# Gate and up half passes of three units in one run, in shared pairs of PSUM banks

## The chip, the core and the metric

The kernel runs on one core of a Trainium2 chip. The metric is device time in microseconds (us) of one execution. The granted TensorE clock was 1.000 in the profiled execution.

## What is computed

`x` is 2048 x 448. Its layer norm `xn` goes through two branches that are added to `x`: a GFNet filter (a two-dimensional FFT, a product with a complex weight, the inverse FFT) and a gated ReLU feed-forward layer with 1792 hidden columns.

```python
xn = _layernorm(x)
X = rfft2(xn) * (w_r + 1j * w_i)
y = irfft2(X, s=(S, D))                     # S = 2048, D = 448
gate = einsum("bsd,df->bsf", xn, W_gate)    # F = 1792
up = einsum("bsd,df->bsf", xn, W_up)
h = gate * (gate > 0) * up
return x + y + einsum("bsf,fd->bsd", h, W_down)
```

## The kernel before

Every product runs in fp16 with each operand split into a high and a low part, so that one product of fp32 operands costs three matmuls (high by high, high by low, low by high).

**Units.** The hidden columns are cut into 14 slabs `f` of 128, the 2048 rows into 4 chunks `q` of 512 (order `CHUNKS`). A gate and up unit is one (`f`, `q`): two accumulations of 128 x 512, gate in one PSUM bank and up in the next, in one tile named `gu` of shape 128 x 2 x 512 (one bank holds 512 fp32). The slabs stand in three groups of 5, 5 and 4. That makes 56 units, listed in `gseq` by group, chunk and slab. When all slabs of a group are done for a chunk, four down blocks follow (`dn_mm`), each 128 rows by 448 columns in a PSUM tile `dn`, with 15 matmuls in groups of five slabs and 12 in the group of four.

**Full and half passes.** The contraction over 448 takes, with the splits, ten full passes of 128 rows and one of 64 rows for gate, and the same for up (`gu_full`, L729, 20 matmuls for a unit; `gu_half`, L736, two). A half pass uses half of TensorE's rows. The gate half pass stands in rows 0 to 63, the up half pass in rows 64 to 127 (`TOP`), so the two run side by side.

**Runs.** Half passes of two units stand together. Units are taken in pairs (lead, mate): after the 20 full passes of the lead, `gu_halves` opens the mate's PSUM tile, issues the mate's two half passes with `start`, so they open its accumulation, and then the lead's two with `stop`, so they close it. The mate's 20 full passes follow later. That is a run of four half passes, and 28 such runs in the program.

**PSUM.** There are eight banks: two tiles `gu` of two banks, two tiles `dn` of one bank, two tiles `fx` of one bank for all FFT products.

**Who reads the tiles.** `gu_relu` (ScalarE, L766) reads the gate bank, `gu_times` (VectorE, L770) the up bank; `dn_post` (VectorE, L803) reads a down block and adds it to the result tile `xy`. Only after that can a tile's banks be written again by their next tenant. `gu_hi` (L774) and `gu_lo` (L778) make the fp16 parts `h` for the down blocks.

**What sets the order.** The first 44 us or so follow a list written by hand (`OPENING`); its entries `hp0`, `hp2`, `hp4` are the runs of half passes of the first units. After that a scheduler orders each engine's queue when the program is built: among instructions that its model of the chip finds ready it takes the one of highest priority. Half passes have a raised priority (an offset of 2000) except the first of a run, and each is tied to the one before it in order (`tc.add_manual_dep`, a tie of order, not a wait). FFT work (forward L358 and L399, inverse L619 and L647, and much of VectorE's work) is spread between the units as background. TensorE works its queue off in that order, so once built, nothing moves ahead of a wait.

Of the kernel before, what the change touches and what calls it, by code (L numbers as in the profile page):

```python
# [10 lines left out]
F32 = mybir.dt.float32  # L11
# [11 lines left out]
VT = XW + 14  # L23
GROUPS = [5, 5, 4]
LAG, AHEAD, RAMP = 1, 3, 6
NWARM = 19
N2ORD = [0, 8, 4, 12, 2, 10, 6, 14, 1, 9, 5, 13, 3, 11, 7, 15]
CHUNKS = [0, 2, 1, 3]
# [128 lines left out]
def tile_gfnet_reglu(ctx: ExitStack, tc: tile.TileContext, x, xr, wgu, wd, wf, ident, c_fd, c_fm, c_im, c_row, c_id,  # L157
# [5 lines left out]
    psum = ctx.enter_context(tc.tile_pool(name="psum", bufs=1, space=bass.MemoryType.PSUM))  # L163

    def mt(shape, dt, name, bufs=1):
        return main.tile(shape, dt, name=name, bufs=bufs)
# [44 lines left out]
    state = {}  # L211
# [506 lines left out]
    hps, ht = {}, {}  # L718

    SEQ = [(r + 4 * k, r) for r in range(3) for k in (0, 1)] + [(t, 4 + t) for t in range(3)] + [(3, 3)]  # L720
    TOP = ((slice(0, 64), 3), (slice(64, 128), 7))

    def gu_open(f, q):
        hps[f, q] = psum.tile([128, 2, 512], F32, name="gu", bufs=2)

    def gu_full(f, q, gs, cs, start, stop, seq=SEQ):
        for g in gs:
            for i, (a, b) in enumerate(seq):
                last["P"] = P.matmul(hps[f, q][:, g, cs], wt[f, g][:, a, :], Tq[q][:, b, cs],  # L729
                                     start=(start and i == 0), stop=(stop and i == len(seq) - 1)).ins  # L730

    def gu_half(f, q, g, start, prev):


        rows, b = TOP[g]
        m = P.matmul(hps[f, q][:, g, 0:512], wt[f, g][rows, 7, :], Tq[q][rows, b, :], start=start, stop=not start).ins  # L736
        if "opened" in state:
            tc.add_manual_dep(m, prev.name, NOSYNC, reason="half passes stand together")
        return m

    NOSYNC = mybir.DependencyInfo(mybir.DependencyClass.NoSync, mybir.DependencyReason.DATA)
    opened = set()

    def gu_unit(f, q, mate):

        gs, cs = (0, 1), slice(0, 512)
        if (f, q) in opened:
            gu_full(f, q, gs, cs, False, True)
            return
        gu_open(f, q)  # L750
        gu_full(f, q, gs, cs, True, False)
        gu_halves(f, q, mate)

    def gu_halves(f, q, mate):
        gu_open(*mate)
        m = last["P"]
        for i in range(4):
            with tc.high_priority(offset=2000 if i else 0):
                m = gu_half(*((f, q) if i > 1 else mate), 1 - i % 2, i < 2, m)
        opened.add(mate)  # L760

    g1s = {}

# [16 lines left out]
    def gu_post(f, q):  # L780
        gu_relu(f, q)
        gu_times(f, q)
        gu_hi(f, q)
        gu_lo(f, q)
# [4 lines left out]
    def dn_mm(fs, n2):  # L789
        q, j = n2 % 4, n2 // 4  # L790
        js = slice(128 * j, 128 * (j + 1))
        ps = psum.tile([128, 512], F32, name="dn", bufs=2)
        n = 3 * len(fs)
        i = 0
        for f in fs:
            for a, b in ((0, 0), (0, 1), (1, 0)):
                last["P"] = P.matmul(ps[:, 0:D], ht[f, q][:, a, js], wdt[f][:, b, :], start=(i == 0),  # L797
                                     stop=(i == n - 1)).ins
                i += 1
        dps[n2] = ps  # L800

    def dn_post(g, n2):
        last["V"] = V.scalar_tensor_tensor(xy[:, n2, :], dps[n2][:, 0:D], dsc[:, g:g + 1], xy[:, n2, :],  # L803
                                           op0=OP.mult, op1=OP.add).ins

    def store(n2):

        if n2 in stored:
            nc.sync.dma_start(ov[:, n2, :], xy[:, n2, :])
        stored.add(n2)  # L810
# [111 lines left out]
    for t in range(16 + len(il) - 1):  # L922
# [4 lines left out]
        for st in reversed(range(len(il))):  # L927
            i = t - st
# [14 lines left out]
    def run_bg(until=None, amount=0.0):  # L943
        credit[0] += amount
        while pos[0] < len(bg) and (credit[0] > 0 if until is None else pos[0] < until):
            c, p, fn, a = bg[pos[0]]
            bg_item(fn, a)
            pos[0] += 1
            credit[0] -= c - load[0] * p
# [3 lines left out]
    for n in GROUPS:  # L953
        groups.append(list(range(f0, f0 + n)))
        f0 += n
    gseq = [("gu", g, f, q) for g, fs in enumerate(groups) for q in CHUNKS for f in fs]
    units, pend = [], []
    for k, u in enumerate(gseq):
        units.append(u)
        if k % 2 and pend:  # L960
            units += pend
            pend = []
        if u[2] == groups[u[1]][-1]:
            pend = [("dn", u[1], u[3] + 4 * j, None) for j in range(4)]
    units += pend
    mates = {u: v for u, v in zip(gseq[::2], gseq[1::2])}
    first = {}
    for i, u in enumerate(units):
        if u[0] == "gu" and u[2] not in first:
# [49 lines left out]
    def keep_warm(n):  # L1019
        for _ in range(n):  # L1020
            P.matmul(wps, warm[:, 0:128], warm, start=True, stop=True)

    pieces = {"lid": lambda: nc.sync.dma_start(id_t, ident), "lfd": lambda: nc.sync.dma_start(fd_t, c_fd),
              "lw": load_wn, "warm": lambda: keep_warm(NWARM),
              **{f"kw{n}": (lambda n=n: keep_warm(n)) for n in (1, 3, 6)},
# [3 lines left out]
    def piece(name, fn, *a):  # L1029
        pieces[name] = lambda: fn(*a)  # L1030
# [14 lines left out]
    q = CHUNKS[0]  # L1045

    def gu_slab(f, g):
        if f % 2 == 0 and g == 0:
            gu_open(f, q)
        gu_full(f, q, (g,), slice(0, 512), f % 2 == 0, f % 2 == 1)  # L1050

    for f in groups[0]:
        piece(f"lwd{f}", load_wd, f)
        piece(f"wdq{f}", wd_sq, f, f)
        piece(f"wdh{f}", wd_hi, f, f)
        piece(f"wdl{f}", wd_lo, f, f)
        piece(f"parW{f}", w_sum, f)
        piece(f"wscW{f}", w_scale, f)
        for tag, fn in (("re", gu_relu), ("tm", gu_times), ("gh", gu_hi), ("gl", gu_lo)):
            piece(f"{tag}{f}", fn, f, q)  # L1060
        if f % 2 == 0:
            piece(f"hp{f}", gu_halves, f, q, mates["gu", 0, f, q][2:])
        for g in range(2):
            piece(f"wsqW{f}g{g}", w_sq, f, g)
            piece(f"whiW{f}g{g}", w_hi, f, g)
            piece(f"wloW{f}g{g}", w_lo, f, g)
            piece(f"gu{f}g{g}", gu_slab, f, g)
            if f == 0:
                piece(f"parW{f}g{g}", w_sum, f, (g,))
                piece(f"wscW{f}g{g}", w_scale, f, (g,))  # L1070
                for h in range(2):
                    for tag, sq in (("hh", seq1[0:3]), ("lh", seq1[3:6]), ("hl", seq2)):
                        piece(f"{tag}{g}{h}", gu_full, f, q, (g,), half[h], tag == "hh" and h == 0, False, sq)

    with tc.manual_schedule(engines={mybir.EngineType.PE, mybir.EngineType.DVE, mybir.EngineType.Activation,
                                     mybir.EngineType.SP, mybir.EngineType.Pool}):
        A.activation(mt([128, 1], F32, "root"), eps, AF.Sqrt)
        G.memset(warm, 0.0)
        wps = psum.tile([128, 512], F32, name="dn", bufs=2)
        gu_open(0, q)  # L1080
        for name in OPENING.split():
            pieces[name]()
# [12 lines left out]
    def room(i, share):  # L1095
        return max(0.0, share * took(units[i]) - fixed(i))
# [4 lines left out]
    for _ in range(40):  # L1101
        m = (lo + hi) / 2
# [5 lines left out]
    @contextmanager  # L1108
    def after(i):
        k = max(0, len(anchors) - 1 - i)  # L1110
        with tc.issue_after(anchors[k]), tc.issue_after(act_anchors[k]):
            yield

    for i, u in list(enumerate(units))[len(groups[0]):]:
        is_gu = u[0] == "gu"
        if is_gu:
            _, g, f, q = u
            run_bg(until=marks["T", q])
            gu_unit(f, q, (mates.get(u) or (0, 0, None, None))[2:])
        else:  # L1120
            _, g, n2, _ = u
            dn_mm(groups[g], n2)
        with after(LAG):
            for fn, a in at.get(i, []):
                with tc.high_priority(offset=200):
                    fn(*a)
            for v in units[i + 1:i + 1 + AHEAD]:
                if v[0] == "gu":
                    run_bg(until=marks["T", v[3]])
            run_bg(amount=room(i, load[0]) if i >= RAMP else 0.0)  # L1130
        if is_gu:
            with tc.high_priority(offset=400):
                gu_post(f, q)
        else:
            with tc.high_priority(offset=400):
                dn_post(g, n2)
            if g == len(groups) - 1:
                store(n2)
        anchors.append(last["V"])
        act_anchors.append(last["A"])  # L1140
# [46 lines left out]
```

## Time and profile before

| what | value |
|---|---|
| time, median of 3 runs | 455.11 us (454.88 to 455.12) |
| the profiled execution | span 453.5 us from the first to the last instruction; its own time is not listed, and the runs' median is 1.6 us above its span |
| TensorE (PE) busy | 445.2 us, 98% of the span, 2613 matmuls |
| VectorE (DVE) busy | 383.6 us, 85% |
| ScalarE (ACT) busy | 188.0 us, 41% |
| GpSimd (POOL) busy | 22.5 us, 5% |
| granted TensorE clock | 1.000 |

In the profile's rows PE is TensorE's matmuls and PEld its weight loads, DVE is VectorE, ACT ScalarE. Rows of the timeline give the start, the length from the first start to the last end, engine, line, operation, tile written and tiles read, shapes and the count of matmuls merged into the row. Matmuls are pipelined: a row's length includes the drain of its last matmul, so the pace is read from one row's start to the next row's start. Rows of the groups give the count, the busy time, the mean ns of one, and after the bar the engine's idle time before them with what ended it.

### The profile page before, as it was taken

Reading aid. Unit: us, or ns where it says so; the run is one execution under the profiler, and the core shown is the slowest. Engines: PE = TensorE matmul, PEld = TensorE weight load, DVE = VectorE, ACT = ScalarE, POOL = GpSimd, SP = SyncE. Lnnn points to the kernel's source line nnn. Section 1 sums busy time; section 2 is a strip of 40 time slices with the busy share of each in tenths; the row PEclk is TensorE's granted clock in tenths of the full one; section 3 lists DMA queues with packets and bytes.
Section 4 is the critical chain, followed back from the end, with each engine's and each line's share of the span. In section 5 each row is a group of like instructions: output and inputs, shape, how many; then the busy total and the mean of one; then the engine's idle time right before and its main releaser. Section 6 shows DMA issues by size and latency. Waiting matters only on the chain.

```text
span 453.5 us, 7307 instructions
## 1 busy us (share of the span) xinstructions
PE 445.2 (98%) x2613; PEld 224.9 (50%) x2613; DVE 383.6 (85%) x931; ACT 188.0 (41%) x406; POOL 22.5 (5%) x73
## 2 busy tenths in 40 slices
PE   7999999999999999999999999999999999999996
PEld 2544645555555444444444444444555656655642
DVE  5999798979769799999999999996996989875522
ACT  4896233542544575143124345433263344243020
POOL 2220020100000040000000000000000000000000
PEclk9999999999999999999999999999999999999999
DMA  7939983130001462341320200002210211110202
GB/s 255 324 71 283 382 252 65 25 70 2 1 1 48 138 195 71 92 144 41 88 58 21 82 21 2 0 1 81 68 59 24 93 52 63 58 35 1 103 20 81
DMA packets 36908, 39.39 MB, mean 87 GB/s; under 512 B 16278, under 2 KB 32534, under 8 KB 36872
## 3 DMA queue, kind: packets, MB, share of 16 engines
q1 hardware_dynamic: 36872, 38.93, 27.8%
q8 instruction: 20, 0.33, 0.3%
q14 instruction: 16, 0.13, 0.1%
HBM read 24.69 MB, written 3.67 MB: 63 GB/s over the span
## 4 chain that ended last, share of the span: by engine, by line
PE 95%; DVE 2%; DMA 1%; ACT 1%; SPq 0%; issue 0%
PE gu L729 53%; PE dn L797 28%; PE gu L736 3%; PE fx L647 3%; PE fx L358 3%; PE fx L619 2%; PE fx L399 2%; DMA y<-in_xr 1%; ACT wt L679 0%; ACT T L344 0%; DVE xy L803 0%; DVE bst L261 0%; DVE tt L323 0%; SPq L237 0%; SPq L231 0%
## 5 line engine op out<-in xcount | busy, mean ns | idle before, releaser
L729 PE MATMUL gu<-T,wt 128*128 128x512 f16 (+1 forms) x1140 | 255.3, 375 | 0.0
L729 PEld LDWEIGHTS <-wt 128*128 128x128 f16 x1140 | 109.2, 98 | 128.5 <-issue 8.1
L797 PE MATMUL dn<-wdt,h 128*128 128x448 f16 x672 | 136.4, 352 | 0.6 <-DVE xy L803 0.6
L797 PEld LDWEIGHTS <-h 128*128 128x128 f16 x672 | 65.3, 98 | 61.1 <-issue 1.3
L766 ACT ACTIVATE g<-gu 128x512 f32<-128x512 f32 x56 | 33.3, 595 | 119.2 <-PE gu L736 87.5
L770 DVE SCALAR_TENSOR_TENSOR g<-gu,g 128x512 f32<-128x512 f32 x56 | 38.4, 686 | 23.7 <-ACT g L766 23.4
L774 ACT ACTIVATE h<-g 128x512 f16<-128x512 f32 x56 | 34.9, 626 | 51.3 <-DVE g L770 51.3
L778 DVE TENSOR_TENSOR h<-g,h 128x512 f16<-128x512 f32 x56 | 38.3, 685 | 7.9 <-ACT h L774 7.5
L803 DVE SCALAR_TENSOR_TENSOR xy<-dn,dsc,xy 128x448 f32<-128x448 f32 x48 | 32.4, 678 | 10.8 <-PE dn L797 10.8
L679 ACT ACTIVATE wt<-wst,wsc 128x512 f16<-128x512 f32 x28 | 19.0, 714 | 5.0 <-DVE wsc L207 5.0
L635 ACT ACTIVATE pgh<-pg 114x512 f16<-114x512 f32 x16 | 10.1, 630 | 25.3 <-PE fx L647 20.5
L683 DVE SCALAR_TENSOR_TENSOR wt<-wst,wsc,wt 128x512 f16<-128x512 f32 x28 | 20.3, 745 | 0.1
L197 ACT ACTIVATE junk<-wst 128x512 bf16<-128x512 f32 x28 | 17.5, 623 | 1.9 <-DMA wst<-in_wgu 1.6
L736 PE MATMUL gu<-T,wt 64*128 64x512 f16 x112 | 17.0, 381 | 0.2 <-DVE wt L683 0.2
L647 PE MATMUL fx<-idc_t,pgh 114*128 114x112 f16 (+1 forms) x192 | 16.6, 236 | 0.0
L647 PEld LDWEIGHTS <-pgh 114*128 114x128 f16 x192 | 13.9, 98 | 3.8 <-issue 0.8
L406 DVE TENSOR_TENSOR y<-y,y 128x456 f32<-128x456 f32 x22 | 13.9, 630 | 2.3 <-DMA row<-y 1.8
L652 DVE SCALAR_TENSOR_TENSOR xy<-fx,fsc,xy 128x448 f32<-128x448 f32 x16 | 10.8, 678 | 5.4 <-PE fx L647 5.4
L200 POOL PARTITION_ALL_REDUCE wm<-wm x15 | 6.2, 416 | 176.9 <-ACT junk L197 161.0
L603 ACT ACTIVATE vt<-y,fsc 128x456 f16<-128x456 f32 x16 | 10.8, 672 | 9.2 <-DMA y<-row 5.4
L405 DVE TENSOR_TENSOR y<-y,y 128x456 f32<-128x456 f32 x22 | 13.8, 628 | 0.2
L390 ACT ACTIVATE Xh<-X 128x456 f16<-128x456 f32 x16 | 9.2, 577 | 11.2 <-DVE X L388 6.8
(118 smaller groups left out, 453.7 us busy)
## 6 DMA issues: line engine op xcount, KB each, us to landing
sw<-y SPq DMA_DIRECT2D x64, 112.2 KB
wst<-in_wgu SPq DMA_DIRECT2D x28, 256.0 KB
wf<-in_wf SPq DMA_DIRECT2D x16, 228.0 KB
y<-in_xr SPq DMA_DIRECT2D x16, 224.0 KB
xy<-in_x SPq DMA_DIRECT2D x16, 224.0 KB
out<-xy SPq DMA_DIRECT2D x16, 224.0 KB
wdst<-in_wd SPq DMA_DIRECT2D x14, 224.0 KB
fm<-in_c_fm SPq DMA_DIRECT2D x4, 256.0 KB
```

What stands on the lines that cost most here:

```text
L197: A.activation(mt([128, 512], BF16, "junk")[:, 0:src.shape[-1]], src, AF.Square, scale=SQ, accum_out=acc)
L647: P.matmul(ps[:, o0:o1], h[:, a, i, :], idc_t[:, b, c0:c0 + o1 - o0], start=(j == 0 and i < 3), stop=True, skip_group_check=True)
L679: A.activation(w[:, 0:4, :], wst[f, g], AF.Copy, scale=wsc[f, g])
L683: V.scalar_tensor_tensor(w[:, 4:8, :], st, sc, w[:, 0:4, :], op0=OP.mult, op1=OP.subtract)
L729: last["P"] = P.matmul(hps[f, q][:, g, cs], wt[f, g][:, a, :], Tq[q][:, b, cs], start=(start and i == 0), stop=(stop and i == len(seq) - 1 ...
L736: m = P.matmul(hps[f, q][:, g, 0:512], wt[f, g][rows, 7, :], Tq[q][rows, b, :], start=start, stop=not start).ins
L766: last["A"] = A.activation(g1s[f, q], hps[f, q][:, 0, :], AF.Relu, scale=2.0 ** -22).ins
L770: last["V"] = V.scalar_tensor_tensor(g1, hps[f, q][:, 1, :], 2.0 ** -22, g1, op0=OP.mult, op1=OP.mult).ins
L774: A.activation(ht[f, q][:, 0, :], g1s[f, q], AF.Copy)
L778: V.tensor_tensor(h[:, 1, :], g1s.pop((f, q)), h[:, 0, :], op=OP.subtract)
L797: last["P"] = P.matmul(ps[:, 0:D], ht[f, q][:, a, js], wdt[f][:, b, :], start=(i == 0), stop=(i == n - 1)).ins
L803: last["V"] = V.scalar_tensor_tensor(xy[:, n2, :], dps[n2][:, 0:D], dsc[:, g:g + 1], xy[:, n2, :], op0=OP.mult, op1=OP.add).ins
```

## The change

Units are now taken in batches: 2, 2, then sixteen of 3, then 2, 2 (56 units, 20 batches). The first unit of a batch is the lead, the others are its mates. `gu_halves` opens each mate's tile and issues its two half passes, mate by mate, and the lead's two at the end; all but the very first have the raised priority. The pool `gu` has three tiles of two banks; the pool `dn` is gone, and two down blocks share one `gu` tile, one bank each (`pair_of_banks`). The warm-up matmuls at the start use one such tile as well. Down blocks that are due are put after the end of a batch. Nothing is added or left out: each engine has the same number of instructions as before.

```diff
+BATCHES = [2, 2]
...
+    def pair_of_banks():
+        return psum.tile([128, 2, 512], F32, name="gu", bufs=3)
+
     def gu_open(f, q):
-        hps[f, q] = psum.tile([128, 2, 512], F32, name="gu", bufs=2)
+        hps[f, q] = pair_of_banks()
...
-    def gu_halves(f, q, mate):
-        gu_open(*mate)
+    def gu_halves(f, q, mates):
         m = last["P"]
-        for i in range(4):
-            with tc.high_priority(offset=2000 if i else 0):
-                m = gu_half(*((f, q) if i > 1 else mate), 1 - i % 2, i < 2, m)
-        opened.add(mate)
+        for i, v in enumerate([*mates, (f, q)]):
+            mate = i < len(mates)
+            if mate:
+                gu_open(*v)
+                opened.add(v)
+            for g in (1, 0):
+                with tc.high_priority(offset=0 if not i and g else 2000):
+                    m = gu_half(*v, g, mate, m)
...
     def dn_mm(fs, n2):
...
-        ps = psum.tile([128, 512], F32, name="dn", bufs=2)
+        if j % 2 == 0:
+            state["dn"] = pair_of_banks()
+        ps = state["dn"][:, j % 2, :]
...
+    batches = BATCHES + [3] * ((len(gseq) - sum(BATCHES) - 4) // 3) + [2, 2]
+    assert sum(batches) == len(gseq)
+    lead, ends = {}, set()
+    for n in batches:
+        k = len(ends) and max(ends) + 1
+        lead[gseq[k]] = [v[2:] for v in gseq[k + 1:k + n]]
+        ends.add(k + n - 1)
     units, pend = [], []
     for k, u in enumerate(gseq):
         units.append(u)
-        if k % 2 and pend:
+        if k in ends and pend:
...
-        wps = psum.tile([128, 512], F32, name="dn", bufs=2)
+        wps = pair_of_banks()[:, 0, :]
```

How the built order moves is shown at one place, the third chunk of the second group of slabs (row tile `T1`), on TensorE's queue. Ahead of the change, the unit `gu_2935` is the lead and `gu_2956` its mate (`wt` are weights, `T1` the rows; the number in a name tells tiles apart):

```order
L729 LDWEIGHTS wt_2042
L729 MATMUL gu_2935<-T1_64,wt_2042 128x512
L736 LDWEIGHTS wt_2095
L736 MATMUL gu_2956<-T1_64,wt_2095 128x512
L736 LDWEIGHTS wt_2090
L736 MATMUL gu_2956<-T1_64,wt_2090 128x512
L736 LDWEIGHTS wt_2042
L736 MATMUL gu_2935<-T1_64,wt_2042 128x512
L736 LDWEIGHTS wt_2037
L736 MATMUL gu_2935<-T1_64,wt_2037 128x512
L729 LDWEIGHTS wt_2090
L729 MATMUL gu_2956<-T1_64,wt_2090 128x512
```

The four half passes stand in one run, the lead's full passes ahead of it, the mate's behind it.

With the change, at the same place the batch has the lead `gu_2878` and the mates `gu_2899` and `gu_2902`; `gu_2827` ahead of them is a tile of two down blocks. After the lead's 20 full passes come 30 matmuls of down blocks, and then:

```order
L806 LDWEIGHTS h_2738
L806 MATMUL gu_2827<-wdt_2550,h_2738 128x448
L740 LDWEIGHTS wt_2033
L740 MATMUL gu_2899<-T1_64,wt_2033 128x512
L740 LDWEIGHTS wt_2028
L740 MATMUL gu_2899<-T1_64,wt_2028 128x512
L733 LDWEIGHTS wt_2028
L733 MATMUL gu_2899<-T1_64,wt_2028 128x512
```

and 20 full passes of `gu_2899` later:

```order
L733 MATMUL gu_2899<-T1_64,wt_2033 128x512
L740 LDWEIGHTS wt_2095
L740 MATMUL gu_2902<-T1_64,wt_2095 128x512
L740 LDWEIGHTS wt_2090
L740 MATMUL gu_2902<-T1_64,wt_2090 128x512
L740 LDWEIGHTS wt_1970
L740 MATMUL gu_2878<-T1_64,wt_1970 128x512
L740 LDWEIGHTS wt_1965
L740 MATMUL gu_2878<-T1_64,wt_1965 128x512
L733 LDWEIGHTS wt_2090
L733 MATMUL gu_2902<-T1_64,wt_2090 128x512
```

The six half passes of the batch stand in two runs here, one of two and one of four, with the first mate's full passes between them. So it is in 15 of the 16 batches of three, with 2 to 20 full passes or other work between; in the sixteenth, the one that `OPENING` places, the six stand in one run. The four batches of two have runs of four. That makes 35 runs in the built order, 20 of four or six half passes and 15 of two.

On VectorE's queue at the same place the read of the down block that frees the tile of `gu_2899` stands as follows (`xy` is the result, the lines ahead of it are background FFT work; the first row reads the other tile's first block):

```order
L812 SCALAR_TENSOR_TENSOR xy_61<-gu_2827,dsc_90,xy_61 128x448
L537 TENSOR_TENSOR y2_68<-y2_68,sw2_1921 128x4x57
L538 TENSOR_TENSOR y2_68<-y2_68,sw2_1921 128x4x57
...
L429 SCALAR_TENSOR_TENSOR y16_82<-y4_70,y5_71 128x456
L430 SCALAR_TENSOR_TENSOR y5_71<-y4_70,y5_71 128x456
L504 TENSOR_TENSOR y4_70<-y1_67,wf_2382 128x456
L505 TENSOR_TENSOR y1_67<-y1_67,wf_2382 128x456
L506 TENSOR_TENSOR y4_70<-y4_70,y1_67 128x4x57
L507 TENSOR_TENSOR y4_70<-y4_70,y1_67 128x4x57
L504 TENSOR_TENSOR y1_67<-y11_77,wf_2384 128x456
L505 TENSOR_TENSOR y11_77<-y11_77,wf_2384 128x456
L812 SCALAR_TENSOR_TENSOR xy_61<-gu_2780,dsc_90,xy_61 128x448
```

Left out in it are two more rows like the second and third. Before, a mate's tile was never freed by a down block, since down blocks had banks of their own; now the half passes of a mate wait for this read, the tile `gu_2780` being the former tenant of `gu_2899`'s banks.

More of the change, by code (lines that the diff above doesn't have):

```diff
@@ L742, in tile_gfnet_reglu, with gu_unit @@
     opened = set()
-    def gu_unit(f, q, mate):
+    def gu_unit(f, q, mates):
         gs, cs = (0, 1), slice(0, 512)
@@ L751, in gu_unit @@
         gu_full(f, q, gs, cs, True, False)
-        gu_halves(f, q, mate)
-    def gu_halves(f, q, mate):
-        gu_open(*mate)
+        gu_halves(f, q, mates)
+    def gu_halves(f, q, mates):
         m = last["P"]
-        for i in range(4):
-            with tc.high_priority(offset=2000 if i else 0):
-                m = gu_half(*((f, q) if i > 1 else mate), 1 - i % 2, i < 2, m)
-        opened.add(mate)
+        for i, v in enumerate([*mates, (f, q)]):
[6 more added lines that the diff above has]
+                    m = gu_half(*v, g, mate, m)
     g1s = {}
@@ L965, in tile_gfnet_reglu @@
     units += pend
-    mates = {u: v for u, v in zip(gseq[::2], gseq[1::2])}
     first = {}
@@ L1061, in tile_gfnet_reglu @@
         if f % 2 == 0:
-            piece(f"hp{f}", gu_halves, f, q, mates["gu", 0, f, q][2:])
+            piece(f"hp{f}", gu_halves, f, q, lead["gu", 0, f, q])
         for g in range(2):
@@ L1118, in tile_gfnet_reglu @@
             run_bg(until=marks["T", q])
-            gu_unit(f, q, (mates.get(u) or (0, 0, None, None))[2:])
+            gu_unit(f, q, lead.get(u))
         else:
```

## Prediction

> **What bounds the kernel now.** I read the page's busy times first, then the chain that ended last, then who TensorE waits for, then its timeline around the half passes.
>
> ```profile
> PE 445.2 (98%) x2613; PEld 224.9 (50%) x2613; DVE 383.6 (85%) x931; ACT 188.0 (41%) x406; POOL 22.5 (5%) x73
> core 0: 453.5 us, clock 1.000
> PE 95%; DVE 2%; DMA 1%; ACT 1%; SPq 0%; issue 0%
> PE fx L338 <- DVE tt L323: 1.8, 2, 1.5
> PE dn L1021 <- POOL warm L1078: 1.5, 1, 1.5
> PE dn L797 <- DVE xy L803: 0.6, 1, 0.6
> PE fx L338 <- ACT wt L679: 0.5, 1, 0.5
> PE gu L736 <- DVE wt L683: 0.2, 1, 0.2
> ```
>
> TensorE makes up 95% of the chain. The last five rows are all its waits: 4.6 us, of which all but the 0.6 at L803 belong to the transposes, the warm-up and the first weights at the start. From there to the last chunk it never stands still for another engine. So the time is TensorE's instruction stream plus what is lost between two instructions of that stream, and the change leaves the stream's matmuls as they are in kind and number. What remains is what a run of half passes costs beyond its own passes. The timeline of TensorE shows it:
>
> ```profile
> 29.92 8.81 PE L729 MATMUL gu<-T,wt 128*128 128x512 f16 x40
> 38.66 0.60 PE L736 MATMUL gu<-T,wt 64*128 64x512 f16 x4
> 38.88 0.38 PE L736 MATMUL gu<-T,wt 64*128 64x512 f16 x2
> 39.20 4.49 PE L729 MATMUL gu<-T,wt 128*128 128x512 f16 x20
> 43.52 0.54 PE L797 MATMUL dn<-wdt,h 128*128 128x448 f16 x2
> ...
> 251.88 5.84 PE L797 MATMUL dn<-wdt,h 128*128 128x448 f16 x30
> 257.56 0.59 PE L729 MATMUL gu<-T,wt 128*128 128x512 f16 x2
> 258.08 0.61 PE L736 MATMUL gu<-T,wt 64*128 64x512 f16 x4
> 258.62 4.49 PE L729 MATMUL gu<-T,wt 128*128 128x512 f16 x20
> 262.95 1.68 PE L797 MATMUL dn<-wdt,h 128*128 128x448 f16 x8
> ```
>
> (The third row is a narrow window on the second half of the run in the second.) A full pass has a pace of 0.216 us: 20 of them from 39.20 to 43.52 and again from 258.62 to 262.95. Forty take 8.64, but from 29.92 to the run at 38.66 it is 8.74: **0.10 is lost going in**. At 257.56 two take 0.43, but the run starts 0.52 later: 0.09. The run's first pair starts at 38.66, its second at 38.88: 0.22, the pace of one full pass, so the two half passes of a pair run side by side, and nothing to speak of is lost between pairs. From the second pair at 38.88 to the next full pass at 39.20 is 0.32, which is **0.10 lost going out**. A run of four so takes 0.54 (258.08 to 258.62 as well) where its two passes are worth 0.43, and with the way in it loses 0.21. That holds with a down block ahead or behind:
>
> ```profile
> 277.90 4.48 PE L729 MATMUL gu<-T,wt 128*128 128x512 f16 x20
> 282.31 0.61 PE L736 MATMUL gu<-T,wt 64*128 64x512 f16 x4
> 282.85 5.85 PE L797 MATMUL dn<-wdt,h 128*128 128x448 f16 x30
> 288.54 8.80 PE L729 MATMUL gu<-T,wt 128*128 128x512 f16 x40
> ```
>
> In: 4.41 less 4.32 is 0.09; the run 0.54. Going in and out is paid once a run, however many pairs stand in it. The 28 runs lose 28 x 0.21 = 5.9 us, the largest loss in TensorE's stream.
>
> **The change, part by part.**
>
> *Runs of half passes.* Read from the code, 28 runs become 20 batches, worth 8 x 0.21 = 1.7 us. The built order says otherwise. In 15 of the 16 batches of three, the first mate's pair stands alone, other work follows, and the second mate's pair comes later with the lead's: two runs in place of one. So there are 20 runs of two or three pairs and 15 of a single pair, 35 in all, seven more than before. A run of three pairs costs what one of two does, by the 0.22 between pairs. A run of one pair is not in the trace. Bounds: nothing, if a lone pair could be slipped in free, and 0.21, as for a run of two. I take 0.20, 0.10 in and 0.10 out, since both losses stand at the borders of a run and the borders are the same. Sum: 20 x 0.21 + 15 x 0.20 = 7.2 against 5.9, so **+1.3 us**; with 0.21 for all, 7 x 0.21 = +1.5. I take **+1.4**.
>
> [...]
>
> *PSUM: three pairs that down blocks share.* `gu_times` and `dn_post` cost the same; what changes is who waits for them. A mate's pair now waits for the down block that last held its banks. VectorE works a long queue, and reads late:
>
> ```profile
> 174.36 4.51 PE L797 MATMUL dn<-wdt,h 128*128 128x448 f16 x23
> 178.71 3.19 PE L729 MATMUL gu<-T,wt 128*128 128x512 f16 x14
> 182.47 0.68 DVE L803 SCALAR_TENSOR_TENSOR xy<-dn,dsc,xy 128x448 f32<-128x448 f32 x1
> L803 DVE SCALAR_TENSOR_TENSOR xy<-dn,dsc,xy 128x448 f32<-128x448 f32 x48 | 32.4, 678 | 10.8 <-PE dn L797 10.8
> DVE  5999798979769799999999999996996989875522
> L536 DVE TENSOR_TENSOR y<-y,sw 128x228 f32<-128x228 f32 x32 | 12.4, 386 | 0.8 <-issue 0.7
> L503 DVE TENSOR_TENSOR y<-y,wf 128x456 f32<-128x456 f32 x16 | 10.1, 631 | 0.4
> ```
>
> The block that ended at 178.71 was read by 183.15, 4.4 us later. The shortest handover in the new order is the one shown for `gu_2899`: between the last matmul of the block in `gu_2780` and the half pass stand only the 15 matmuls of the next block, 15 x 0.189 (30 from 251.88 to 257.56) = 2.8 us. Bounds: no wait, and 4.4 - 2.8 = 1.6 us. I take none. VectorE's queue there: from the first block of `gu_2827` on, whose read can start when its matmuls end, come that read, 12 steps of background and the read that counts, half the steps as wide as L503 and half as L536: 0.68 + 6 x 0.63 + 6 x 0.39 + 0.68 = 7.5 us. TensorE in that time does 20 full passes and 30 matmuls of down blocks, 20 x 0.216 + 30 x 0.189 = 10.0. The read is due 2.5 us ahead, unless a DMA of the swaps or of `wf`, which four of these steps read, is late. All other mates' handovers leave 3.4 us or more.
>
> *Second block of a pair.* It waits for the read of the first, since the two share a tile. The order puts a block of the other tile between them, as two tiles `dn` were used in turn before. At the end of the program TensorE's last 24 instructions of down blocks stand and wait as before, so the one wait there stays:
>
> ```profile
> 439.84 4.70 PE L797 MATMUL dn<-wdt,h 128*128 128x448 f16 x24
> 445.13 4.70 PE L797 MATMUL dn<-wdt,h 128*128 128x448 f16 x24 [0.59 <-DVE xy L803]
> ```
>
> Bounds: -0.6 if it went, +0.6 if another like it came at each end of a group; taken as 0.
>
> *Warm-up in a shared pair, the order on ScalarE, VectorE, POOL and SP.* Costed at nothing: the same instructions, and their cover is TensorE's stream, which waited for none of them after the start. If that cover is gone at one place, it costs what the handover above does. SP and POOL issue the same DMAs in nearly the same order. The third batch needs the pair that the last warm-up wrote or the first units left, both long free.
>
> *Sum.* +1.4 on the profiled execution: span 453.5 to 454.9. The median lies 1.6 above that execution's span, so 455.1 + 1.4 = **456.5**.
>
> **The rivals.**
>
> 1. *The split runs cost 1.4 and the handovers stall as well.* For it: the read that came 4.4 us late, and VectorE's row of 40 slices of 11.3 us, 9 in each from the 15th to the 27th, 159 to 306 us. Against: the count of its queue above, and that TensorE had no such wait before. Price 1.6 at one place: 458.1; two or three places with half of that would be near 459.
>
> 2. *The loss is one for each pair, not for each run.* In the trace every run has two pairs, so the sum could be 56 x 0.106, and 56 pairs stay 56: 455.1. Against: the losses stand at the borders, 0.09 to 0.10 each, and the pairs inside follow at the pace of full passes.
>
> 3. *A lone pair slips in free.* Two half passes side by side fill all 128 rows like a full pass; if such a pair between full passes lost nothing, 20 x 0.21 = 4.2 against 5.9 gives -1.7: 453.4, faster. The point from which it decides is 15 x c = 5.9 - 4.2, c = 0.11 for a lone pair: below it the kernel gains. Against: the way out costs 0.10 after a pair whatever stands ahead of it, and so does the way in.
>
> 4. *The change does what it says,* 20 runs: 453.4 too. The built order excludes it; TensorE takes its queue in order.
>
> **How the numbers follow.** A measurement of this kernel tells 0.2% (0.9 us) from no change. Chances: the forecast 0.69, rival 1 0.16, rival 2 0.08, rival 3 0.05, others 0.02. The forecast's own range is 456.0 to 456.9, from the bounds 1.3 and 1.5 and the spread of the runs; a tenth of it, with a small gain elsewhere, could fall within 0.2%. Faster 0.06, same 0.13, slower 0.81. The range leaves out rival 3 and most of rival 2 below and the dearer part of rival 1 above: 455.6 to 458.3.
>
> **What would show it.** In the profile after: L740 in 35 runs, 15 of them with two half passes, each 0.31 to 0.32 from its first start to the next full pass and 0.10 late behind the work ahead; the runs of six 0.75 long. TensorE's waits in the middle of the program absent, and 0.6 at L812 at the end. Rival 1 shows as waits of L740 on L812 or L777; rivals 2 and 3 as lone pairs with next to no loss. The prediction is wrong if VectorE's reads stall TensorE in several batches, or if a lone pair costs much other than 0.20.

## Result and the profile after

The changed kernel takes 456.26 us (median of 6 runs, 455.75 to 456.63) against 454.93 us for the kernel before beside it (6 runs, 454.81 to 455.12): 1.3 us more, a ratio of 1.0031 (95% interval 1.0019 to 1.0042). The forecast was 456.5 us, its range 455.6 to 458.3.

The page after, its busy row and the shares of the chain, then everything TensorE waited for (us in total, times, longest):

```profile
PE 445.5 (98%) x2613; PEld 224.6 (49%) x2613; DVE 384.7 (85%) x931; ACT 186.7 (41%) x406; POOL 27.3 (6%) x73
PE 95%; DVE 2%; DMA 1%; ACT 1%; SPq 0%; issue 0%
PE fx L339 <- DVE tt L324: 1.5, 2, 1.2
PE gu L1036 <- POOL warm L1093: 1.5, 1, 1.5
PE fx L339 <- ACT tt L307: 1.1, 1, 1.1
PE gu L806 <- DVE xy L812: 0.6, 1, 0.6
PE fx L339 <- ACT wt L680: 0.5, 1, 0.5
PE gu L740 <- DVE wt L684: 0.2, 1, 0.2
```

TensorE still makes the time, and it waits only in the opening and once at the end. No half pass (L740) waits for a bank: its one wait is for the first weights, as before. So the time is in TensorE's own stream. The busy row and the waits do not say so by themselves: PE is busy only 0.3 us longer (445.2 before) and waits 0.8 us longer (4.6 before, 5.4 after). That is the opening. The 19 warm-up matmuls took less time than before, and TensorE waited longer behind them:

```profile
1.49 7.19 PE L1021 MATMUL dn<-warm 128*128 128x512 f16 x19 [1.49 <-POOL warm L1078]
1.49 5.81 PE L1036 MATMUL gu<-warm 128*128 128x512 f16 x19 [1.49 <-POOL warm L1093]
8.37 0.51 PE L339 MATMUL fx<-id_t,tt 128*128 128x128 f16 x6 [1.08 <-ACT tt L307]
20.11 0.60 PE L736 MATMUL gu<-T,wt 64*128 64x512 f16 x4 [0.18 <-DVE wt L683]
19.66 0.61 PE L740 MATMUL gu<-T,wt 64*128 64x512 f16 x4 [0.18 <-DVE wt L684]
```

(The first and the fourth row are of the kernel before, the others of the changed one.) From the first run of half passes to the last instruction it is 433.4 us before (20.11 to 453.5) and 434.9 after (19.66 to 454.5): 1.5 us more, with the one wait of 0.6 at the end in both. The timeline after, at two batches of three:

```profile
225.90 2.54 PE L733 MATMUL gu<-T,wt 128*128 128x512 f16 x11
228.37 0.39 PE L740 MATMUL gu<-T,wt 64*128 64x512 f16 x2
228.69 2.55 PE L733 MATMUL gu<-T,wt 128*128 128x512 f16 x11
231.17 0.60 PE L740 MATMUL gu<-T,wt 64*128 64x512 f16 x4
231.71 1.47 PE L733 MATMUL gu<-T,wt 128*128 128x512 f16 x6
...
266.81 1.03 PE L733 MATMUL gu<-T,wt 128*128 128x512 f16 x4
267.77 0.39 PE L740 MATMUL gu<-T,wt 64*128 64x512 f16 x2
268.09 1.90 PE L733 MATMUL gu<-T,wt 128*128 128x512 f16 x8
269.92 0.61 PE L740 MATMUL gu<-T,wt 64*128 64x512 f16 x4
270.46 0.82 PE L733 MATMUL gu<-T,wt 128*128 128x512 f16 x3
```

The lone pair at 228.37 follows eleven full passes that are worth 11 x 0.216 = 2.38 us and took 2.47: 0.09 going in. From its start to the next full pass is 0.32, of which 0.216 is its own pass: 0.10 going out. The next eleven take 2.48 to the run of four, 0.10 more than they are worth, and that run again 0.54. The lone pair loses as much as the run of four.

### The profile page after: what moved, and what is told of

Read it like the earlier page. It is cut to its first block, busy times and chain, and to the rows that moved or that the text cites. A ratio compares the mean times of both kernels' runs of the same rounds, so it can differ in the third digit from the quotient of the medians.

```text
span 454.5 us, 7317 instructions
## 1 busy us (share of the span) xinstructions
PE 445.5 (98%) x2613; PEld 224.6 (49%) x2613; DVE 384.7 (85%) x931; ACT 186.7 (41%) x406; POOL 27.3 (6%) x73
## 4 chain that ended last, share of the span: by engine, by line
PE 95%; DVE 2%; DMA 1%; ACT 1%; SPq 0%; issue 0%
PE gu L733 53%; PE gu L806 28%; PE gu L740 3%; PE fx L648 3%; PE fx L359 3%; PE fx L620 2%; PE fx L400 2%; DMA y<-in_xr 1%; ACT T L345 0%; DVE xy L812 0%; ACT wt L680 0%; DVE bst L262 0%; DVE tt L324 0%; SPq L238 0%; SPq L232 0%
## 5 line engine op out<-in xcount | busy, mean ns | idle before, releaser
L806 PE MATMUL gu<-wdt,h 128*128 128x448 f16 x672 | 134.0, 352 | 0.6 <-DVE xy L812 0.6
L812 DVE SCALAR_TENSOR_TENSOR xy<-gu,dsc,xy 128x448 f32<-128x448 f32 x48 | 32.4, 679 | 17.0 <-PE gu L806 17.0
L740 PE MATMUL gu<-T,wt 64*128 64x512 f16 x112 | 18.2, 383 | 0.2 <-DVE wt L684 0.2
L201 POOL PARTITION_ALL_REDUCE wm<-wm x15 | 7.9, 524 | 145.2 <-ACT junk L198 145.2
L537 DVE TENSOR_TENSOR y<-y,sw 128x228 f32<-128x228 f32 x32 | 12.4, 389 | 1.5 <-DMA sw<-y 1.5
(118 smaller groups left out, 455.6 us busy)
```

## Experiments

How many runs of half passes a kernel has is counted in its built order and in its profile.

**Batches of two with the shared banks.** It takes the shared banks alone, without the batches of three.

```diff
-    batches = BATCHES + [3] * ((len(gseq) - sum(BATCHES) - 4) // 3) + [2, 2]
+    batches = [2] * (len(gseq) // 2)
```

> The changed kernel with batches of two only: three shared pairs of PSUM banks, but 28 runs of four half passes as before the change. Theory (a run costs 0.21 us at its two borders, and the shared banks cost nothing): 28 runs, so the time of the kernel before, 454.9 us, within 0.4. Rival (the shared banks, with down blocks and mates waiting for each other, carry part of the 1.3 us): 455.5 to 456.3 us with 28 runs.

Measured: 454.81 us against 454.70 for the kernel before, ratio 1.0001 (0.9992 to 1.0010). Its profile has 28 runs of four, each as before:

```profile
225.77 2.11 PE L733 MATMUL gu<-T,wt 128*128 128x512 f16 x9
227.80 0.61 PE L740 MATMUL gu<-T,wt 64*128 64x512 f16 x4
228.34 4.92 PE L733 MATMUL gu<-T,wt 128*128 128x512 f16 x22
```

The three shared pairs of banks cost and bring nothing that can be measured (by the interval, at most some 0.4 us either way). What the change costs lies in the batches of three.

**Every unit's pair alone.**

```diff
-    batches = BATCHES + [3] * ((len(gseq) - sum(BATCHES) - 4) // 3) + [2, 2]
+    batches = BATCHES + [1] * (len(gseq) - sum(BATCHES))
```

> The changed kernel with batches of one unit after the first four: each unit's pair of half passes stands alone at its own end, 54 runs (2 of four, 52 of two). Theory (0.21 us for each run, whatever its length): 54 x 0.21 = 11.4 against 5.9 us before, so 454.9 + 5.5 = 460.4 us. Rival (the loss is one for each pair, and 56 pairs stay 56): 454.9 us. Rival (a lone pair is cheaper than a run of two, say half): 52 x 0.11 + 0.4 = 6.1, about 455.1 us.

Measured: 460.35 us, ratio to the kernel before 1.0125 (1.0111 to 1.0139), 5.7 us by that ratio. The forecast was 5.5. Its timeline, with a lone pair between full passes and FFT work:

```profile
399.83 1.67 PE L733 MATMUL gu<-T,wt 128*128 128x512 f16 x7
401.44 0.39 PE L740 MATMUL gu<-T,wt 64*128 64x512 f16 x2
401.76 1.04 PE L648 MATMUL fx<-idc_t,pgh 114*128 114x112 f16 x12
```

In: 1.61 less 7 x 0.216 = 1.51 is 0.10; out 0.32 less 0.216 is 0.10, though what follows is small. The loss is one for each run and not for each pair, which rules out the rival of one loss a pair, and a lone pair isn't cheap, which rules out the rival that slips it in free.

**Half passes over all rows.**

```diff
-        rows, b = TOP[g]
+        rows, b = slice(0, 128), TOP[g][1]
```

> The changed kernel in its own order, with each half pass run over all 128 rows of TensorE (its sums then hold products that do not belong there), so no two run side by side and the row tiling never changes. Theory (the borders are the switch between 128-row and 64-row tiling): 35 borders' 7.4 us go, 56 passes of 0.216 us = 12.1 come, 456.3 + 4.7 = 461.0 us, and the next pass follows at 0.216 us on both sides of a run. Rival (the loss is that of opening and closing an accumulation in another bank, not of the tiling): 456.3 + 12.1 = 468.4 us, with 0.31 still at the borders.

Measured: 461.02 us, ratio to the kernel before 1.0138 (1.0122 to 1.0153).

```profile
299.71 0.38 PE L740 MATMUL gu<-T,wt 128*128 128x512 f16 x1
299.93 10.52 PE L733 MATMUL gu<-T,wt 128*128 128x512 f16 x48
310.29 0.59 PE L740 MATMUL gu<-T,wt 128*128 128x512 f16 x2
310.72 1.46 PE L733 MATMUL gu<-T,wt 128*128 128x512 f16 x6
```

The passes that open and close accumulations in the same banks, in the same places, now follow at the common pace: 48 from 299.93 to 310.29 are 0.216 each, and two from 310.29 to 310.72 take 0.43. (The first row is the last pass of a run of four, at the edge of the window.) The loss is gone at all borders (461.02 us measured, where the sum without it is 461.0), so it belongs to going from 128 to 64 rows and back, not to the banks or to opening and closing a sum. Running side by side is not it either, since inside a run the pairs follow each other at 0.22 us.

The weight loads (PEld) show one thing more that goes with it, in the changed kernel (first two rows) and with all rows (last two):

```profile
228.37 0.10 PEld L740 LDWEIGHTS <-wt 64*128 64x128 f16 x2 [0.42 <-issue]
228.69 0.76 PEld L733 LDWEIGHTS <-wt 128*128 128x128 f16 x5 [0.23 <-issue]
310.07 0.31 PEld L740 LDWEIGHTS <-wt 128*128 128x128 f16 x2
310.50 0.53 PEld L733 LDWEIGHTS <-wt 128*128 128x128 f16 x3
```

With all rows the weights of the passes at 310.29 and 310.72 start to load 0.22 us ahead of them. At the borders of the changed kernel the load starts together with its pass, at 228.37 and at 228.69, and so at every border of it, 0.005 us ahead or less. The traces put 0.10 us at each change between 128 and 64 rows and 0.01 us or less between the pairs of one run; whether the weight load that is not ahead makes the 0.10 us or only goes with it, no run here separates.

**All six together.** `reads` holds the reads that free a pair of banks (`gu_times`, `dn_post`; the last line stands in both), in program order, and `SYNC` makes the tie a wait.

```diff
+    SYNC = mybir.DependencyInfo(mybir.DependencyClass.Sync, mybir.DependencyReason.DATA)
...
             for g in (1, 0):
                 with tc.high_priority(offset=0 if not i and g else 2000):
                     m = gu_half(*v, g, mate, m)
+                if not i and g and len(mates) > 1 and "opened" in state:
+                    tc.add_manual_dep(m, reads[-1].name, SYNC, reason="half passes wait for the last pair")
...
+        reads.append(last["V"])
```

> The changed kernel with one more dependency: the first half pass of a batch of three also waits for the read that frees the last pair of banks, so that all six half passes stand together; the built order has 20 runs, 16 of six and 4 of four. Theory: 20 x 0.21 = 4.2 against 5.9 us before and 7.4 after, so 453.2 us, 1.7 below the kernel before and 3.2 below the changed one. Rival (the later start of the run stalls TensorE where the second mate's banks came free after the lone pair had started, by 1.0 and 1.5 us at two places where the order offers little else): 454.2 to 455.7 us, with waits of the half passes for VectorE in the profile.

Measured: 454.66 us, ratio 1.0001 (0.9992 to 1.0010). The theory's 453.2 did not come; the rival did, in kind and in time, though with three waits where it had two. What TensorE's half passes waited for in its profile, and the longest of the three waits, on TensorE and on VectorE:

```profile
PE gu L740 <- DVE xy L817: 1.6, 3, 1.0
187.05 1.24 PE L733 MATMUL gu<-T,wt 128*128 128x512 f16 x5
189.33 0.82 PE L740 MATMUL gu<-T,wt 64*128 64x512 f16 x6 [1.04 <-DVE xy L817]
188.60 0.68 DVE L817 SCALAR_TENSOR_TENSOR xy<-gu,dsc,xy 128x448 f32<-128x448 f32 x1
```

The run of six is 0.76 from 189.33 to the next full pass at 190.09, three passes and one loss, as the theory has it. But at 189.33 it had waited for the read of the last banks, which ended at 189.28. By the pace of starts the runs at 69.19, 189.33 and 254.12 came 0.27, 1.11 and 0.46 us later than a run without a wait, 1.8 us together, and they eat up the 1.7 us that eight runs fewer are worth. All three stand behind down blocks that had the last banks. At the other twelve, the run of six waited for nothing.

**Together where the banks are free.** The same kernel, with the dependency left out in those three batches.

```diff
-                if not i and g and len(mates) > 1 and "opened" in state:
+                if not i and g and len(mates) > 1 and "opened" in state and (f, q) not in ((2, 2), (7, 0), (6, 1)):
```

> As the kernel that holds the six half passes of a batch together, but without the added dependency in the three batches where its profile showed TensorE waiting for the read of the last banks (leads: slab 2 of chunk 2, slab 7 of chunk 0, slab 6 of chunk 1); those three stay split. The built order has 23 runs, 13 of six, 3 lone pairs, 7 of four. Theory (0.21 us for each run, no waits left): 23 x 0.21 = 4.9 against 5.9 us before, 454.7 - 1.0 = 453.7 us, faster than both kernels, and no wait of a half pass for VectorE in the profile. Rival (the order built without those ties moves the reads and stalls at other batches): 454.4 us or more, with such waits.

Measured: 453.86 us against 454.75 for the kernel before, ratio 0.9981 (0.9972 to 0.9990): 0.9 us faster than before, some 2.3 us faster than the changed kernel by the two ratios. TensorE's waits of down blocks and half passes in its profile (the others are the transposes and the warm-up at the start), and the batch at 228.37 of the changed kernel, with VectorE's read of the last banks:

```profile
PE gu L811 <- DVE xy L817: 0.6, 1, 0.6
PE gu L740 <- DVE wt L684: 0.2, 1, 0.2
225.66 1.67 PE L733 MATMUL gu<-T,wt 128*128 128x512 f16 x7
227.36 0.82 PE L740 MATMUL gu<-T,wt 64*128 64x512 f16 x6
228.12 5.14 PE L733 MATMUL gu<-T,wt 128*128 128x512 f16 x23
226.63 0.68 DVE L817 SCALAR_TENSOR_TENSOR xy<-gu,dsc,xy 128x448 f32<-128x448 f32 x1
```

The table names no wait of a half pass for the read of a down block any more. The six half passes stand together at 227.36, while the changed kernel issued the lone pair at 228.37 and the rest at 231.17. They start 1.70 us after seven passes worth 1.51; of the 0.19 between, 0.10 is the way in, and the other 0.1 is a wait that the table doesn't name: the read of the last banks ended at 227.31. By the starts it is the only one, and too small to be told in the time. So in twelve of the fifteen split batches the chip did not force the split: the six half passes can stand together there for 0.1 us of waiting in all. That the builder's model frees the banks later than the chip does is the reason I see for it; no run shows it.

**The kernel before once more.**

> The kernel before, unchanged, for a second profile. If the start of the first half passes (20.1 us before, 19.5 to 19.9 us in the five profiles with shared banks) is set by when the first rows of the input arrive, it varies here too and lies between 19.4 and 20.2 us; if the shared banks bring it forward, it is 20.1 again.

Measured: 455.07 us in one run. Its first run of half passes starts at 19.88 us, without shared banks:

```profile
19.88 0.60 PE L736 MATMUL gu<-T,wt 64*128 64x512 f16 x4 [0.18 <-DVE wt L683]
```

That start was 20.11 in the first profile of the same kernel and lies between 19.45 and 19.90 in the six others. So two executions of one program differ here by 0.2 us; what sets it was not tried.

The number of runs and the time, by the ratios to the kernel before (454.7 us):

| kernel | runs | by 0.21 us a run | measured |
|---|---|---|---|
| together where free | 23 | -1.1 | -0.9 |
| batches of two, shared banks | 28 | 0 | 0.0 |
| changed kernel | 35 | +1.5 | +1.4 |
| every pair alone | 54 | +5.5 | +5.7 |

Two kernels have a second term beside the runs. All six together has 20 runs, worth -1.7, and 1.8 us of waits: 0.0 measured. With all rows the 5.9 us of the runs go and 56 passes of 0.216 us come, +6.2: +6.3 measured.

## Why the prediction came out

*What bounds.* Right. TensorE's queue makes up 95% of the chain that ended last in seven of the eight profiles, and it loses time inside its own stream. In the kernel with all six together it is 73%, and VectorE 21%: there the half passes wait for VectorE's reads.

*The runs of half passes.* Right, and the term that decided: read from the code, the change takes eight runs away; read from the built order, it adds seven. Sized +1.3 to +1.5, with 0.20 for a lone pair. By the starts of single matmuls, a lone pair loses what a run of four does, so the upper end, +1.5, is the stream's own difference.

*The span.* It was forecast to grow by 1.4 us and grew from 453.5 to 454.5, by 1.0: 1.5 in the stream, less the 0.45 by which the first half passes came earlier. The prediction had nothing for the opening. As the second profile of the kernel before shows, about half of the 0.45 can be one execution against another; the rest stays open. That the medians, 1.3 us apart, came so near to +1.4 is in part luck.

*The handovers.* Costed at nothing, and nothing they cost, but the margin was mis-sized. At `gu_2899` the read was forecast 2.5 us ahead of the half pass. TensorE and VectorE after:

```profile
243.66 4.48 PE L733 MATMUL gu<-T,wt 128*128 128x512 f16 x20
250.81 3.00 PE L806 MATMUL gu<-wdt,h 128*128 128x448 f16 x15
253.74 0.39 PE L740 MATMUL gu<-T,wt 64*128 64x512 f16 x2
245.63 0.68 DVE L812 SCALAR_TENSOR_TENSOR xy<-gu,dsc,xy 128x448 f32<-128x448 f32 x1
252.06 0.68 DVE L812 SCALAR_TENSOR_TENSOR xy<-gu,dsc,xy 128x448 f32<-128x448 f32 x1
```

The block ended at 250.81 and its read at 252.74, 1.0 us ahead of the half pass. The steps between the two reads took 6.4 us (245.63 to 252.06; counted 6.8), but the first read itself started 2.0 us after its block had ended at 243.66. I had counted VectorE's queue from that read on as if it were free for it, and it was behind already. The first rival's mechanism is real where less stands between, as the kernel with all six together shows.

*The second block of a pair, the end.* Right: 0.6 us at the end, before and after.

*The warm-up.* Its 19 matmuls took 7.19 and 6.88 us in the two profiles of the kernel before and 5.81 to 7.08 in the six with shared banks. Whether the shared banks have a part in that was not tried; with batches of two (7.08) the time is that of the kernel before.

*The rivals.* One loss for each pair and a free lone pair are refuted by the kernel with every pair alone. That the change does what it says stayed excluded by the order; the kernel that holds the passes together where the banks are free comes nearest to it and gives 0.9 of the 1.7 us, with 23 runs.

## What to carry to other kernels

Where an engine takes its queue in order, count a change's effect in the order that is built, not in the loop that asks for it: here the code asked for 20 runs, the builder made 35, and TensorE ran 35 in the profile. A scheduler can split what should stand together; tie such a group to the last of its releases, then look in the profile for the places where that release is really late, and untie only those. A busy share of 98% does not tell that an engine loses nothing: the rows of passes overlap (0.38 us long, one every 0.22), so a loss of 0.10 at a border counts as busy time (445.2 us before, 450.5 with every pair alone). A comparison of starts with the pace shows it.

## What was not expected of the hardware

In these traces the loss at a border doesn't depend on what stands at the other side: 0.10 us towards matmuls of 512 columns, and 0.10 towards FFT products of 112 (401.76 in the kernel with every pair alone). By the single starts a border costs 0.096 us at the first pass behind it and 0.010 more at the second, 0.226 where 0.216 is the pace: some 0.106 in all, and 0.21 for the two borders of a run.
